# Two of the first unit's seven classical chunks mixed by block products, and their token-matrix groups narrowed in earlier chunks

## The chip, the cores and the metric

The kernel runs on one core of one Trainium2 chip. The metric is the device time of one execution in microseconds (us); lower is better. A core has TensorE (PE, with its weight loads shown as PEld), VectorE (DVE), ScalarE (ACT), GpSimd (POOL) and SyncE (SP), which here issues most of the DMAs.

## The reference

`x` is 8 x 3008 x 256. The first half is a spectral layer (transform along the 3008 tokens, complex 256x256 mix, soft threshold, transform back); the second is a mixer block on its result `y`:

```python
X = np.fft.rfft(x, axis=1)
Yr = Xr @ w_r - Xi @ w_i + b_r
Yi = Xr @ w_i + Xi @ w_r + b_i
Yr, Yi = soft_threshold(Yr, 0.01), soft_threshold(Yi, 0.01)
y = np.fft.irfft(Yr + 1j * Yi, n=3008, axis=1)
...
h = np.maximum(y.T @ w_tok1, 0) @ w_tok2      # along tokens, 256 wide inside
u = y + h.T
out = u + np.maximum(u @ w_ch1, 0) @ w_ch2    # along channels, 1536 wide inside
```

## The kernel before, in words

Batches are taken in five units: batch 0, batch 1, and three pairs. Of each unit the spectral part (names `p`, `px`, `pm`, `pi`, `gp` on TensorE) must be done before its channel mixing can start. The channel mixing of a unit walks over *chunks* of tokens. A product in full precision is three matmuls of high and low parts (`mm3`).

There are two ways to mix a chunk. A **classical** chunk (`channel(n)`, at most 512 columns) makes, for each of 12 slices f of the inner width, `ph` (6 matmuls), its relu `hh` on ACT with the rest `hlo` on DVE, and `po` (6 matmuls): 144 matmuls of the chunk's width. A **wide** chunk (`channel7`, 940 to 1024 columns) cuts both weight layers and the chunk into quarters and uses seven block products instead of eight (`sx`, `sw`, `sy`, `sz`, `l` on TensorE, operands `op` and `ts` made by DVE, ACT and POOL): 6 pairs of slices x 2 layers x 7 products x 3 = 252 matmuls of half the chunk's width. In `channel7` the order of TensorE is the order of the code.

Before a chunk can be mixed its `u` must be made, by *groups* of 4 or 5 slots (376 or 470 columns) that don't line up with wide chunks. `half_u(g, ct)` is one half of group g: 6 matmuls with the group's token matrix (`wt2`), then small ones with `b2`, 10 rows of the profile for 5 slots. Both `wt2` and `b2` have one buffer each, so the loads of group g+1 go out on SP when group g has been used (`load_group(g + 1)` behind the second half). The table `needs` says which groups a chunk needs; `when` and `spots` in `channel7` say beside which step a half is made: with three groups, the spots for the second wide chunk are behind `N5` and `N7` of the first step, behind `N1` of the next, and then behind whole pairs of slices.

The token matrix comes as 64-bit floats. In the first unit each group is loaded raw, narrowed (`narrow`: 2 operations of ACT and 6 of DVE for each of two halves), split into high and low parts (`split_wt2`: ACT, then DVE) and written back to DRAM by `keep_wt2`; later units reload it from there. The raw tiles share the buffers "ld" (four) with the loads `x` and `a2` of the spectral part, the narrowed ones the buffers "o" with the spectral part's `xh` and `xl`.

The order of the work: a start of 157 us; then the classical chunks of unit 0, between whose slices the driver at the end of the program deals out the spectral steps of unit 1 and some of unit 2, at a `pace` of so much spectral work per classical work; then, before the last classical chunk, all the rest of the spectral work alone ("pure"); then the last classical chunk, in which the block weights are summed (`weigh`, `replace`) and the first groups for the first wide chunk are made; then wide chunks to the end. A scheduler turns this into the order of each engine, so work may be moved by some places. Before, chunks 0 to 6 are classical (470, 376, 376, 376, 470, 470, 470 columns) and chunk 7 (960) is the first wide one.

Of the kernel before, what the change touches and what calls it, by code (L numbers as in the profile page):

```python
# [29 lines left out]
TOKS = 2 * N1  # L30
# [5 lines left out]
NF = DF // 128  # L36
# [101 lines left out]
def tile_kernel(ctx: ExitStack, tc: tile.TileContext, io):  # L138
# [17 lines left out]
    def split(hi, lo, src, hi_eng, lo_eng):  # L156
        if hi_eng is S:
            S.copy(out=hi, in_=src)  # L158
        else:
            hi_eng.tensor_copy(out=hi, in_=src)  # L160
        lo_eng.tensor_tensor(out=lo, in0=src, in1=hi.bitcast(F32), op=ALU.subtract)  # L161
# [59 lines left out]
    wc = {"wt2": wk}  # L221
# [219 lines left out]
    def fetch_g(u):  # L441
        gts[u] = [const.tile([128, 2, len(UNITS[u]), C], F32R, name=n, tag=n) for n in ("gh", "gl")]
        for i, g in enumerate(gts[u]):
            DMA.dma_start(out=g.rearrange("p j b c -> p (j b c)").bitcast(F32), in_=g_d[u][i, :, :2 * len(UNITS[u]) * C])
# [440 lines left out]
    for u, bs in enumerate(UNITS):  # L885
        total, at = N * len(bs), 0
        if u == 0:
            widths = [k * TOKS for k in sizes[u]]
        else:
            widths = [total % CW7] + [CW7] * (total // CW7)  # L890
        for cw in widths:
            chunks.append((u, at, cw))
            at += cw
        assert at == total
# [17 lines left out]
    def load_wt2(g, pool=None, parts=(0, 1)):  # L912
        u, _, s, k = groups[g]
        cols = slice(s * TOKS, (s + k) * TOKS)
        if u == 0:
            for jt in parts:
                wfs.setdefault(g, {})[jt] = load_raw(io["wt2"][0, jt][:, cols], k * TOKS, pool)
        else:
            w = wc["wt2"].tile([128, 4, 480], F32R, name="wt2", bufs=1)
            DMA.dma_start(out=w[:, :, :k * TOKS].bitcast(F32), in_=wt2_d[:, :, cols])  # L920
            wts[g] = w

    def narrow_wt2(g, parts=(0, 1)):
        for jt in parts:
            wfs[g][jt] = load_wide(None, wfs[g][jt].shape[1], raw=wfs[g][jt])

    def keep_wt2(g):
        u, _, s, k = groups[g]
        if u == 0:
            DMA.dma_start(out=wt2_d[:, :, s * TOKS:(s + k) * TOKS], in_=wts[g][:, :, :k * TOKS].bitcast(F32))  # L930

    def split_wt2(g, parts=(0, 1)):
        n = groups[g][3] * TOKS
        if g not in wts:
            wts[g] = wk.tile([128, 4, 480], F32R, name="wt2", bufs=1)
        for jt in parts:
            split(wts[g][:, jt, :n], wts[g][:, 2 + jt, :n], wfs[g].pop(jt), S, V)

    def load_b2(g):
        u, b, s, k = groups[g]  # L940
# [53 lines left out]
    def channel(n):  # L994
# [26 lines left out]
        for f in range(NF + 2):  # L1021
# [11 lines left out]
            if after:  # L1033
                mine = needs[n + 1]
                seven = after[2] > CW
                if f == 1 and seven:
                    yield "rest of it"
                    open_seven()
                    fetch_g(after[0])
                    load_wt2(mine[0])  # L1040
                    load_b2(mine[0])
                if f == 2 and not seven:
# [6 lines left out]
                    replace((0, f // 4))  # L1049
                if seven and f % 4 == 1 and f > 1:  # L1050
                    replace((1, f // 4 - 1))
                first_at, apart = (9 if len(mine) == 1 else 4 if seven else 6), (3 if seven else 4)
                for i, g in enumerate(mine):
                    if not seven and f in (1, 3, 4, 5, 6):
# [73 lines left out]
    def replace(key):  # L1128
        layer, q = key
        if layer == 0:  # L1130
            cols = slice(q * 512, (q + 1) * 512)
            h, l = (wc["w1"][:, k, 0, cols].rearrange("m (p i f) -> m p i f", p=2, i=2)[:, :, 1] for k in range(2))
        else:
            h, l = (wc[k][:, 4 * q:4 * q + 4][:, 0::2, 128:] for k in ("w2h", "w2l"))
        split(h, l, kept.pop(key), S, V)
# [372 lines left out]
```

## Time and profile before

| | |
|---|---|
| median of 3 runs | 2316.3 us (2315.58 to 2317.71) |
| the profiled execution | 2314.35 us, span 2312.2 us |
| PE / PEld busy | 98% / 85% |
| DVE / ACT / POOL busy | 74% / 64% / 60% |
| mean granted clock | 0.997 |
| end of classical chunks 0 to 5 (the `po` sums) | 198.7, 234.5, 277.7, 329.3, 389.7, 450.8 us |
| spectral work alone | about 452 to 850 us |
| last classical chunk; wide chunks | 850 to 907 us; 907 us to the end |

Busy shares are shares of the span. The duration of a matmul in a row overlaps the next one, so matmuls are counted below by the distance of their starts.

### The profile page before, as it was taken

What the parts mean: (1) busy time and instruction counts of PE and PEld (TensorE: products, weight loads), DVE (VectorE), ACT (ScalarE), POOL (GpSimd) and SP (SyncE); (2) the same over time, 40 slices, a digit from 0 to 9 for tenths busy, and PEclk for the clock granted to TensorE, in tenths of its full rate; (3) what the DMA queues carried; (4) which work ended last, traced back from release to release, by engine and by line L of the source; (5) the groups of instructions that cost most, each with busy time, mean ns of one, the idle gap of its engine ahead of it and who ended that gap; (6) DMA issues with size and microseconds to landing.
All of it is one profiled execution on the core that took longest, in us unless ns stands there. A gap on an engine that the chain in (4) does not pass through costs nothing.

```text
span 2312.2 us, 34805 instructions
## 1 busy us (share of the span) xinstructions
PE 2272.1 (98%) x12092; PEld 1975.2 (85%) x12092; DVE 1718.3 (74%) x2806; ACT 1476.5 (64%) x2700; POOL 1387.5 (60%) x1118
## 2 busy tenths in 40 slices
PE   8999999999999999999999999999999999999998
PEld 7769999989989988888988888898888889888876
DVE  7967776577887667777777777777777777777877
ACT  6655454455555445776676777667777766767776
POOL 0000222344553433887787888778788877878885
PEclk9999999999999999999999999999999999999999
DMA  8776566787876542122222212222221122222101
GB/s 219 240 251 182 144 196 196 231 264 246 274 238 211 186 153 89 41 81 69 84 62 69 64 34 69 70 85 62 69 65 43 60 69 85 62 69 64 59 1 37
DMA packets 150957, 277.22 MB, mean 120 GB/s; under 512 B 11077, under 2 KB 95389, under 8 KB 150781
## 3 DMA queue, kind: packets, MB, share of 16 engines
q1 hardware_dynamic: 115241, 208.40, 30.1%
q10 hardware_dynamic: 35540, 66.60, 8.6%
q8 instruction: 96, 1.57, 0.3%
q14 instruction: 80, 0.66, 0.1%
HBM read 177.57 MB, written 97.39 MB: 119 GB/s over the span
## 4 chain that ended last, share of the span: by engine, by line
PE 83%; DVE 9%; DMA 3%; issue 2%; ACT 2%; SPq 1%; POOL 1%; ACTq 0%; DVEq 0%; POOLq 0%
PE l L134 15%; PE sx L134 14%; PE sz L134 11%; PE sy L134 10%; PE sw L134 7%; PE px L497 3%; PE pm L208 2%; PE pm L210 2%; PE pm L209 2%; PE gp L210 1%; PE gp L208 1%; PE gp L209 1%; DMA raw<-in_wt 1%; DVE ts L1216 1%; PE ph L209 1%
## 5 line engine op out<-in xcount | busy, mean ns | idle before, releaser
L1213 POOL TENSOR_TENSOR op<-ts,op 128x512 fp32r<-128x512 f32 (+2 forms) x503 | 638.0, 1290 | 243.5 <-ACT op L1246 239.9
L1246 ACT ACTIVATE op<-ts 128x512 fp32r<-128x512 f32 (+2 forms) x504 | 311.2, 619 | 62.6 <-DVE ts L1216 47.9
L1213 DVE TENSOR_TENSOR uf<-sy,uf 128x512 f32<-128x512 f32 (+2 forms) x232 | 156.1, 673 | 222.5 <-PE sy L134 222.0
L134 PE MATMUL l<-op,ws 128*128 128x512 f32 (+2 forms) x1134 | 314.3, 385 | 0.0
L134 PEld LDWEIGHTS l<-op,ws 128*128 128x128 f32 x1134 | 212.9, 188 | 40.1
L1242 ACT ACTIVATE x<-sx 128x512 f32<-128x512 f32 (+2 forms) x252 | 148.5, 589 | 139.2 <-PE sx L134 138.7
L134 PE MATMUL sx<-ub,w 128*128 128x512 f32 (+2 forms) x756 | 211.2, 388 | 2.0 <-DVE ts L1216 1.2
L134 PE MATMUL sx<-ub,ws 128*128 128x512 f32 (+2 forms) x756 | 209.8, 386 | 0.5 <-ACT x L1242 0.5
L161 POOL TENSOR_TENSOR yl<-z,yh 128x512 fp32r<-128x512 f32 x72 | 96.2, 1336 | 125.8 <-ACT yh L158 121.9
L134 PEld LDWEIGHTS sx<-ub,w 128*128 128x128 f32 x756 | 141.4, 188 | 31.6 <-DVE ts L1216 3.5
L134 PEld LDWEIGHTS sx<-ub,ws 128*128 128x128 f32 x756 | 141.9, 188 | 27.8 <-ACT x L1242 0.9
L1213 POOL TENSOR_TENSOR op<-b,op 128x512 fp32r<-128x512 f32 (+2 forms) x126 | 160.6, 1274 | 0.7 <-ACT op L1246 0.2
L1213 DVE TENSOR_TENSOR x<-sw,x 128x512 f32<-128x512 f32 (+2 forms) x126 | 85.7, 680 | 90.3 <-PE sw L134 89.1
L262 POOL TENSOR_TENSOR sd<-x 120x512 f32<-120x512 f32 x39 | 60.8, 1558 | 151.5 <-DVE xl L161 108.2
L208 PE MATMUL pm<-wmh,xth 128*128 128x256 f32 x504 | 145.5, 289 | 2.9 <-DVE z L541 1.6
L1266 ACT ACTIVATE x<-x 128x512 f32<-128x512 f32 (+2 forms) x126 | 78.6, 624 | 108.5 <-DVE x L1213 108.5
L134 PE MATMUL sy<-op,w2h 128*128 128x512 f32 (+2 forms) x464 | 142.0, 387 | 1.4 <-DVE uf L1213 1.4
L210 PE MATMUL pm<-wmh,xtl 128*128 128x256 f32 x504 | 142.5, 283 | 0.0
L209 PE MATMUL pm<-wml,xth 128*128 128x256 f32 x504 | 142.5, 283 | 0.0
L161 POOL TENSOR_TENSOR xtl<-xs,xth 128x256 fp32r<-128x256 f32 x84 | 69.8, 831 | 105.1 <-ACT xth L158 58.7
L161 POOL TENSOR_TENSOR wt<-aw,wt 128x512 fp32r<-128x512 f32 x12 | 16.3, 1361 | 181.9 <-ACT wt L158 181.9
L506 DVE TENSOR_TENSOR xtl<-px,xth 128x512 fp32r<-128x512 f32 x84 | 57.7, 687 | 71.5 <-ACT xth L505 55.5
(225 smaller groups left out, 6679.0 us busy)
## 6 DMA issues: line engine op xcount, KB each, us to landing
wt<-wt_d SPq DMA_DIRECT2D x28, 940.0 KB, 5.6
x<-in_x SPq DMA_DIRECT2D x39, 480.0 KB, 5.6
a<-a_d SPq DMA_DIRECT2D x36, 512.0 KB, 5.9
wt<-ws_d SPq DMA_DIRECT2D x36, 512.0 KB, 4.8
b_d<-bt ACTq DMA_DIRECT2D x36, 512.0 KB, 5.8
a_d<-a ACTq DMA_DIRECT2D x36, 480.0 KB, 4.1
wt<-wt_d SPq DMA_DIRECT2D x21, 752.0 KB, 5.2
b<-b_d SPq DMA_DIRECT2D x32, 480.0 KB, 6.3
```

The costliest lines, as they stand in the source:

```text
L134: return lambda *args, **kw: self.tc.keep_in_program_order(op(*args, **kw))
L161: lo_eng.tensor_tensor(out=lo, in0=src, in1=hi.bitcast(F32), op=ALU.subtract)
L208: PE.matmul(out, lhsT=wh, rhs=xh, start=start, stop=False, skip_group_check=more)
L209: PE.matmul(out, lhsT=wh, rhs=xl, start=False, stop=False, skip_group_check=more)
L210: PE.matmul(out, lhsT=wl, rhs=xh, start=False, stop=stop, skip_group_check=more)
L262: eng.tensor_tensor(out=sd[:, 0], in0=x[:, 0], in1=x[:, 1], op=ALU.add)
L497: PE.matmul(pt[:, o:o + 128], lhsT=x, rhs=f2cols(2 * kp + ab), start=True, stop=True)
L506: V.tensor_tensor(out=v(xl)[:, 1:], in0=both, in1=v(xh)[:, 1:].bitcast(F32), op=ALU.subtract)
L1213: eng.tensor_tensor(out=out, in0=in0, in1=in1, op=op)
L1242: pins[key] = S.activation(out=t, in_=src, func=func)
L1246: pins[k] = S.activation(out=ops[k][:, 0], in_=v[k] if src is None else src, func=AF.Copy if k[0] == "t" else AF.Relu)
L1266: pins["x2r"] = S.activation(out=v["x2"], in_=v["x2"], func=AF.Relu)
```

## The change

Chunks 5 and 6 of before become one wide chunk 5 of 940 columns, the first wide one. So chunk 4 is now the last classical chunk, the spectral steps are dealt out over chunks 0 to 3 instead of 0 to 5, and chunk 4 makes groups 5 and 6 (of unit 0), where the last classical chunk before made groups 7, 8 and 9 (of unit 1). Groups 5 and 6 are now loaded, narrowed, split and kept beside chunks 1 and 2, in addition to those chunks' own groups, and reloaded from DRAM later. The low parts of the split of all groups but the first move from DVE to POOL.

```diff
         if u == 0:
-            widths = [k * TOKS for k in sizes[u]]
+            widths = [k * TOKS for k in sizes[u][:5]]
+            widths.append(total - sum(widths))
...
     def load_wt2(g, pool=None, parts=(0, 1)):
-        if u == 0:
+        if u == 0 and "seven" not in wc:
...
     def split_wt2(g, parts=(0, 1)):
-            split(wts[g][:, jt, :n], wts[g][:, 2 + jt, :n], wfs[g].pop(jt), S, V)
+            split(wts[g][:, jt, :n], wts[g][:, 2 + jt, :n], wfs[g].pop(jt), S, G if g else V)
...
     def channel(n):
                 if f == 1 and seven:
                     yield "rest of it"
                     open_seven()
-                    fetch_g(after[0])
+                    if after[0] != u:
+                        fetch_g(after[0])
                     load_wt2(mine[0])
                     load_b2(mine[0])
...
+                spare_g = {1: 5, 2: 6}.get(n)
+                if spare_g and f in (6, 8):
+                    load_wt2(spare_g, parts=[f // 2 - 3])
+                if spare_g and f in (8, 10):
+                    narrow_wt2(spare_g, parts=[f // 2 - 4])
+                if spare_g and f in (11, 13):
+                    split_wt2(spare_g, parts=[f // 2 - 5])
+                if spare_g and f == NF + 1:
+                    keep_wt2(spare_g)
+                    del wts[spare_g]
```

Three places show how the instructions move. On TensorE, the first wide chunk before: the stage begins with the seven products of the first step (`sx`, `sw`, `sx`, `sw`, `sy`, `sx`, `sx`), the first of the second layer (`l`) and the first of the next step; then comes the first half of the next group (`sz<-wt`).

```order
L134 MATMUL sx<-ub,w_963 128x480 x3
L134 MATMUL sw<-ub,ws 128x480 x3
L134 MATMUL sx<-ub,ws 128x480 x3
L134 MATMUL sw<-ub,w_963 128x480 x3
L134 MATMUL sy<-ub,w_963 128x480 x3
L134 MATMUL sx<-ub,ws 128x480 x3
L134 MATMUL sx<-ub,w_963 128x480 x3
L134 MATMUL l<-op,w2h 128x480 x2
L134 MATMUL l<-op,w2l 128x480
L134 MATMUL sx<-ub,w_963 128x480 x3
L134 MATMUL sz<-wt_9423,gh 128x470 x2
```

The same engine and place after the change, from the fifth product on (the first half of group 7, on the tile `wt_8939`, stands behind the first two products; `wt_9094` is group 8):

```order
L134 MATMUL sy<-ub,w_963 128x470 x3
L134 MATMUL sx<-ub,ws 128x470 x3
L134 MATMUL sz<-wt_8939,gh 128x470 x2
L134 MATMUL sz<-wt_8939,gl 128x470
L134 MATMUL sz<-wt_8939,gh 128x470 x2
L134 MATMUL sz<-wt_8939,gl 128x470
L134 MATMUL sz<-g_78,b_8941 128x94 x5
L134 MATMUL sx<-ub,w_963 128x470 x3
L134 MATMUL l<-op,w2h 128x470 x2
L134 MATMUL l<-op,w2l 128x470
L134 MATMUL sx<-ub,w_963 128x470 x3
L134 MATMUL sz<-wt_9094,gh 128x470 x2
```

Two halves now stand among the first seven products, and only nine matmuls lie between the last use of group 7 and the first of group 8, whose loads wait for that last use.

On DVE, where chunk 0 ends, before: the sum of chunk 0 (`uf<-po`) stands between the split of one group of unit 1 (`xl`) and the sums of another, with `hlo` of chunk 1 ahead of the next `xl`.

```order
L177 TENSOR_SCALAR wide<-wide 128x376
L179 SCALAR_TENSOR_TENSOR wide<-wide 128x376
L161 TENSOR_TENSOR xl<-sd,xh 120x512
L1076 TENSOR_TENSOR uf<-po,uf 128x2x470
L262 TENSOR_TENSOR sd<-x 120x256
L263 TENSOR_TENSOR sd<-x 120x256
L180 TENSOR_SCALAR wide<-wide 128x376
L1012 SCALAR_TENSOR_TENSOR hlo<-ph,hh 128x376
L161 TENSOR_TENSOR xl<-sd,xh 120x512
```

After:

```order
L262 TENSOR_TENSOR sd<-x 120x256
L263 TENSOR_TENSOR sd<-x 120x256
L161 TENSOR_TENSOR xl<-sd,xh 120x512
L1088 TENSOR_TENSOR uf<-po,uf 128x2x470
L262 TENSOR_TENSOR sd<-x 120x256
L263 TENSOR_TENSOR sd<-x 120x256
L161 TENSOR_TENSOR xl<-sd,xh 120x512
L262 TENSOR_TENSOR sd<-x 120x256
L263 TENSOR_TENSOR sd<-x 120x256
L161 TENSOR_TENSOR xl<-sd,xh 120x512
```

The groups of unit 1 now follow each other with nothing between; on TensorE the products with the `xl` behind the sum come right behind the last `po` of chunk 0.

On TensorE, where chunk 1 ends, before: of its last 18 `po` the middle and the end, followed by `ph` of chunk 2.

```order
L208 MATMUL po<-hh,w2h 128x376
L209 MATMUL po<-hlo,w2h 128x376
L210 MATMUL po<-hh,w2l 128x376
L208 MATMUL po<-hh,w2h 128x376
L209 MATMUL po<-hlo,w2h 128x376
L210 MATMUL po<-hh,w2l 128x376
L208 MATMUL ph<-uh,w_963 128x376
```

After:

```order
L208 MATMUL po<-hh,w2h 128x376
L209 MATMUL po<-hlo,w2h 128x376
L210 MATMUL po<-hh,w2l 128x376
L208 MATMUL p_2212<-xh,f1r 128x512
L209 MATMUL p_2212<-xl,f1r 128x512
L210 MATMUL p_2212<-xh,f1r 128x512
L208 MATMUL p_2217<-xh,f1r 128x512
L209 MATMUL p_2217<-xl,f1r 128x512
L210 MATMUL p_2217<-xh,f1r 128x512
L497 MATMUL px<-f_77,a_2149 128x128 x4
L208 MATMUL po<-hh,w2h 128x376
```

Spectral products of units 2 and 1 now stand between the last `po` of chunk 1.

## The prediction

> **What bounds the kernel now.** I read the page first, then a table by stage, then TensorE's rows where the change puts its hands.
>
> ```profile
> span 2312.2 us, 34805 instructions
> ...
> PE 2272.1 (98%) x12092; PEld 1975.2 (85%) x12092; DVE 1718.3 (74%) x2806; ACT 1476.5 (64%) x2700; POOL 1387.5 (60%) x1118
> ```
>
> The stages (columns: length, then PE, PEld, DVE, ACT, POOL busy, granted clock, DMA share, GB/s):
>
> ```profile
> core 0: us, PE busy (x) PEld busy (x) DVE busy (x) ACT busy (x) POOL busy (x), PEclk, DMA share, GB/s
> ...
> 157.00:452.00 295.00, 288.32 (x1723) 269.58 (x1723) 208.83 (x353) 148.44 (x283) 65.75 (x51) 0.99 0.62 187
> 452.00:849.60 397.60, 394.82 (x2609) 358.53 (x2610) 300.39 (x496) 215.36 (x429) 186.01 (x164) 1.00 0.70 227
> ...
> 907.00:2312.20 1405.20, 1391.92 (x6682) 1180.72 (x6680) 1047.62 (x1643) 987.72 (x1760) 1115.04 (x889) 1.00 0.20 61
> ```
>
> TensorE is the bound in every stage: it idles 6.7 of 295 us beside the classical chunks 0 to 5, 2.8 of 398 us in the spectral work alone. So a matmul taken away is time saved, as long as no new wait of TensorE takes its place. Where the last classical chunk meets the first wide one the distances and the waits are:
>
> ```profile
> 904.52 0.38 PE L208 MATMUL po<-hh,w2h 128*128 128x470 f32 x1
> ...
> 906.87 0.37 PE L210 MATMUL po<-hh,w2l 128*128 128x470 f32 x1
> 907.08 0.82 PE L134 MATMUL sx<-ub,w 128*128 128x480 f32 x3
> ...
> 909.07 0.92 PE L134 MATMUL sx<-ub,ws 128*128 128x480 f32 x3 [0.52 <-ACT x L1242]
> ...
> 912.70 0.91 PE L134 MATMUL sx<-ub,w 128*128 128x480 f32 x3 [0.76 <-DVE sw L1213]
> ...
> 915.23 0.93 PE L134 MATMUL sx<-ub,w 128*128 128x480 f32 x3 [0.62 <-DVE ts L1216]
> 916.00 0.58 PE L134 MATMUL sz<-wt,gh 128*128 128x470 f32 x2
> ...
> 918.30 0.89 PE L134 MATMUL sw<-ub,ws 128*128 128x480 f32 x3
> ...
> 919.68 0.81 PE L134 MATMUL sx<-ub,ws 128*128 128x480 f32 x3
> 920.33 0.81 PE L134 MATMUL sw<-ub,w 128*128 128x480 f32 x3
> ```
>
> From 904.52 to 907.08 stand twelve classical matmuls: 0.213 us each for 470 columns. In the wide chunk three of 480 columns take 0.65 us, 0.217 each, the same per column. So 0.213 is the price of a 470-column matmul of either kind.
>
> **The change part by part.**
>
> *The products.* Two classical chunks of 470 go: 2 x 144 = 288 matmuls. One wide chunk of 940 comes: 252 of 470. That is 36 fewer, 36 x 0.213 = **-7.7 us**, all on the engine that bounds. Scaling the 480-column rows instead (0.212) gives -7.9. The groups' halves only move: one group less in each of two classical chunks, one less in the last one, three more in the wide stage, each as long as before. DVE, ACT and POOL work of the wide chunk stays beside TensorE, as in the other wide chunks, where TensorE is busy 1392 of 1405 us.
>
> *The start of the wide stage.* Before, 27 matmuls from 907.08 to 916.00 take 8.92 us, where 27 x 0.217 = 5.85 would do: 3.07 us are lost to the chain of ACT and DVE on a stage that has just begun (the three waits named, and shorter ones). Now two halves of group 7, 2.3 us each (916.00 to 918.30 is such a half), stand inside this chain and fill those waits: -3.07. But then group 8 is due nine matmuls, 9 x 0.213 = 1.9 us, behind the last use of group 7's single buffers. How long a reload takes shows in the last classical chunk before: the queue of SP, TensorE's rows there, the weight loads' wait, and the landing times.
>
> ```profile
> 878.58 0.57 SPq L920 DMA_DIRECT2D wt<-wt_d  x1
> 879.67 0.33 SPq L942 DMA_DIRECT2D b<-b_d  x1
> ```
>
> ```profile
> 878.39 1.25 PE L965 MATMUL pu<-g,b 96*128 96x94 f32 x10
> 879.42 0.46 PE L208 MATMUL ph<-uh,w 128*128 128x470 f32 x1
> ```
>
> ```profile
> 885.87 0.30 PEld L965 LDWEIGHTS pu<-g,b 96*128 96x128 f32 x2 [0.21 <-DMA b<-b_d]
> ```
>
> ```profile
> wt<-wt_d SPq DMA_DIRECT2D x28, 940.0 KB, 5.6
> ...
> b<-b_d SPq DMA_DIRECT2D x28, 480.0 KB, 6.3
> ```
>
> Call 879.42 the end of the old group, T. The matrix is issued at T-0.84 and lands 5.6 us later, at T+4.8; `b` is issued at T+0.25 and is seen to land at T+6.45, where even 24 matmuls between the groups were just too few (the 0.21). In the new order TensorE comes at T+1.9, or T+2.5 if the chain of the first step still delays the `sx` before it; it waits over 2 us for the matrix, then does six matmuls (1.3 us), then waits for `b` until T+6.45. Without waits `b` would be used at T+1.9+1.3 = T+3.2: **3.25 us** lost, which takes back the 3.07. Behind TensorE, in program order, the whole wide stage is queued, so nothing hides it. Bounds for start and reload together: -3.1 (loads land in time) to +3.3 (the first waits stay as well, at least in part); I take +0.2, since both are read from rows of the same operations.
>
> *The clock.* A short idle time can cost more than itself:
>
> ```profile
> 230.75 0.34 PE L210 MATMUL po<-hh,w2l 128*128 128x376 f32 x1
> 232.64 0.43 PE L208 MATMUL po<-hh,w2h 128*128 128x376 f32 x1 [1.55 <-ACT hh L1011]
> ...
> 234.21 0.52 PE L208 MATMUL ph<-uh,w 128*128 128x376 f32 x1
> 234.52 0.52 PE L209 MATMUL ph<-ul,w 128*128 128x376 f32 x1
> ...
> 238.17 0.33 PE L208 MATMUL ph<-uh,w 128*128 128x376 f32 x1
> 238.34 0.33 PE L209 MATMUL ph<-ul,w 128*128 128x376 f32 x1
> ```
>
> ```profile
> 873.52 0.48 PE L209 MATMUL po<-hlo,w2h 128*128 128x470 f32 x1 [1.41 <-DVE hlo L1012]
> ```
>
> Behind a wait of 1.55 us the starts are 0.31 us apart from 234.21 on, against 0.17 for this width, until about 237.6: some 3.4 us at half speed, 1.7 us lost. Behind one of 1.41 us at 873.52 the distance stays 0.21. The new wait of 2.2 us and its half us for `b` lie above both: I take +1.4 of the 1.7 (bounds 0 and 1.7). The Trainium skill, page "TensorE: Matmul & The Clock Gate", section "What's actually happening", says the clock falls back after an idle window of about 3.4 us; by that neither this wait nor the one below would cost any clock, and the sum would be 3 us lower. The trace differs, with half speed behind 1.55 us.
>
> *The classical stage.* Its spectral work now falls on four chunks instead of six. TensorE's share of it is only moved, and what it needs of DVE comes closer together:
>
> ```profile
> 198.73 1.13 DVE L1076 TENSOR_TENSOR uf<-po,uf 128x940 f32<-128x940 f32 x1
> 199.77 0.41 DVE L262 TENSOR_TENSOR sd<-x 120x256 f32<-120x256 f32 x1
> 200.11 0.42 DVE L263 TENSOR_TENSOR sd<-x 120x256 f32<-120x256 f32 x1
> ...
> 201.21 0.69 DVE L161 TENSOR_TENSOR xl<-sd,xh 120x512 fp32r<-120x512 f32 x1
> ```
>
> ```profile
> 199.59 0.28 PE L208 MATMUL p<-xh,f1r 120*128 120x256 f32 x1
> 199.71 0.28 PE L209 MATMUL p<-xl,f1r 120*128 120x256 f32 x1
> ```
>
> ```profile
> L161 POOL TENSOR_TENSOR yl<-z,yh 128x512 fp32r<-128x512 f32 x72 | 96.2, 1336 | 125.8 <-ACT yh L158 121.9
> ```
>
> ```profile
> L1012 DVE SCALAR_TENSOR_TENSOR hlo<-ph,hh 128x470 fp32r<-128x470 f32 x36 | 23.1, 643 | 18.9 <-ACT hh L1011 18.9
> ...
> L161 DVE TENSOR_TENSOR wt<-wide,wt 128x470 fp32r<-128x470 f32 x6 | 4.7, 776 | 1.6 <-ACT wt L158 1.5
> ...
> L161 DVE TENSOR_TENSOR wt<-wide,wt 128x376 fp32r<-128x376 f32 x6 | 4.1, 686 | 0.6 <-ACT wt L158 0.6
> ```
>
> In bulk DVE still fits. From 208.8 us go 24 `hlo` x 0.643 = 15.4, two sums of 1.13, and 12 low parts (4.7 + 4.1 = 8.8) that move to POOL: 182. The stage shortens by 61.4 (288 x 0.213) and two groups of 4.6 to some 224 us: 81% instead of 71%. POOL has 65.8 us there and gains twelve operations; the nearest POOL row, 128x512, is 1.34 us on the page, 16 us at most. DMA goes from a share of 0.62 to some 0.8, which the spectral stage's 0.70 nearly has.
>
> Locally one place does not fit. At the end of chunk 0 the sum `uf<-po` needs the last `po`, and behind it on DVE stand two `sd` and the `xl` that TensorE wants as its very next matmul but one: from 198.73 those take 1.13 + 0.34 + 0.34 + 0.69, less small overlaps, 2.4 us, so TensorE waits some 2.6 us, and 0.8 more for the next `xl` (each group costs DVE 1.4 us, TensorE 6 x 0.12 = 0.7). With 1.6 for the clock: +5.0. Against it, the 1.55 us wait at the end of chunk 1, with 0.5 of shorter gaps and its 1.7 of clock, goes: spectral products now stand between the `po` there: -3.8. The other waits of the stage I leave as they are. Together **+1.2**, bounds -4 (the new place costs nothing) to +6 (DVE late at several chunk ends).
>
> *Costed at nothing.* Loading, narrowing and splitting groups 5 and 6 is moved, not added; the reload in the last classical chunk stands 24 matmuls behind the group before it, as it did before. The spare loads stand in SP's queue ahead of unit 2's first `x` and unit 1's `a2`; that wait is a rival below.
>
> **Sum.** -7.7 + 0.2 + 1.4 + 1.2 = -4.9 us. On the profiled execution's 2314.35 us that is 2309.4; the median of the runs lies 1.95 us above that execution, so the forecast is **2311.3 us**.
>
> **The rivals.**
>
> *Both new waits stay hidden.* The chain of the first step may hold back the products ahead of group 8, or DVE may be ready at chunk 0's end. For it speak the 24-matmul spacing that cost 0.21 us only; against it that nine matmuls are 3.2 us short. Then -7.7 - 3.1 or -7.7 - 3.8 and some of the rest: about 2306 us. Chance 0.12.
>
> *DVE becomes the bound between classical slices.* 81% in the mean hides stretches above 100%, such as chunk 0's end; three more waits like the one at 230.75, 1.55 + 1.7 with its clock less often, would take back 3 to 6 us: 2312 to 2317, no change that can be told. The page "SBUF — State Buffer" of the Trainium skill, section "SBUF: two separate sides", has POOL and a two-input DVE operation lock each other out; by it the twelve moved operations could cost DVE up to those 16 us again, which is this rival. For it: the thin places above. Against it: the spectral stage runs at 76% of DVE (300 of 398) and TensorE idles only 2.8 us there. Chance 0.39.
>
> *The load buffers run dry, and it is slower.* The spare raw tiles take two of four "ld" buffers in chunks 1 and 2, and SP waits for them in order:
>
> ```profile
> SPq L475 <- DVE wide L181: 13.6, 4, 9.4
> ```
>
> Already now SP's loads of `a2` waited 13.6 us in four waits for narrowing on DVE. Four more spare halves could double that; it decides once a wait outlasts the lead of `a2`, about one step of unit 1 (some 12 us). If 13.6 us came through: 2311.3 + 13.6 = 2325. Against it, none of the present waits, up to 9.4 us, reached TensorE. Chance 0.07.
>
> **How the numbers follow.** Forecast (gain of 4.6 to 8 us) 0.42, first rival 0.12, second 0.39, third 0.07. About 0.2% (4.6 us) can be told from no change, so faster is 0.42 + 0.12 = 0.54, same 0.39, slower 0.07. The range reaches to the first rival, 2306, and to the end of the second, 2317; the forecast's own is 2308.3 to 2311.7.
>
> **What would show it.** Products: 36 fewer matmuls, distances of 0.213. Reload: a wait of over 2 us at the third `sz<-wt` half, put down to the DMA of `wt` or `b`, and half speed behind it. Classical stage: a wait of some 2.6 us for `xl` at the start of chunk 1, none at its end. I am wrong if the classical stage has many waits for DVE or DMA, or if the reload shows no wait.

## The result: 13 us slower, and the profile after

| | before | after |
|---|---|---|
| median, 4 runs each (lowest to highest) | 2316.89 us (2315.58 to 2317.71) | 2329.78 us (2329.05 to 2330.39) |
| the profiled execution | 2314.35 us, span 2312.2 | 2330.39 us, span 2328.6 |

The ratio is 1.0063, with a 95% interval of 1.0051 to 1.0075: slower by 0.6%, where 0.2% faster was forecast and 2317 was the upper end of the range. From the page of the changed kernel, span and busy times:

```profile
span 2328.6 us, 34964 instructions
...
PE 2274.8 (98%) x12056; PEld 1970.2 (85%) x12056; DVE 1749.2 (75%) x2842; ACT 1504.8 (65%) x2754; POOL 1459.6 (63%) x1173
```

TensorE has 36 matmuls fewer, as the arithmetic says, and is busy 2.7 us longer. To find the place, both executions are cut at the same five points of the program: the first `ph`, the first `ph` of the last classical chunk, the first `sx`, and one and the same `sx` of a later wide chunk. Columns as in the stage table above. Before, then after:

```profile
0.00:156.91 156.91, 140.97 (x786) 117.03 (x786) 121.53 (x253) 100.97 (x184) 3.23 (x6) 0.99 0.82 239
156.91:849.64 692.73, 683.26 (x4332) 628.24 (x4333) 509.31 (x848) 363.89 (x711) 251.80 (x215) 1.00 0.67 210
849.64:907.08 57.44, 56.03 (x296) 49.24 (x295) 39.89 (x65) 23.92 (x46) 17.42 (x9) 1.00 0.46 144
907.08:1372.44 465.36, 463.20 (x2246) 395.22 (x2244) 342.42 (x541) 327.59 (x589) 366.51 (x294) 1.00 0.21 62
1372.44:2312.20 939.76, 928.65 (x4437) 785.44 (x4436) 705.13 (x1102) 660.13 (x1172) 748.53 (x596) 1.00 0.20 60
```

```profile
0.00:161.42 161.42, 142.51 (x787) 117.60 (x787) 122.94 (x254) 101.05 (x184) 3.23 (x6) 0.98 0.82 235
161.42:793.75 632.33, 617.00 (x3981) 566.07 (x3982) 489.90 (x805) 347.45 (x683) 269.76 (x227) 0.99 0.71 226
793.75:850.76 57.01, 52.80 (x264) 44.48 (x263) 41.77 (x67) 23.04 (x43) 19.04 (x9) 1.00 0.41 128
850.76:1388.70 537.94, 533.54 (x2593) 456.71 (x2591) 389.43 (x616) 372.99 (x674) 418.15 (x337) 1.00 0.21 64
1388.70:2328.60 939.90, 928.94 (x4436) 785.28 (x4436) 705.15 (x1102) 660.29 (x1172) 749.41 (x596) 1.00 0.20 60
```

Each row is read against the TensorE work that was moved, at 0.2133 us for a 470-column matmul and 4.6 us for a group (two halves of 2.3):

| stretch | length after minus before | work moved | left over |
|---|---|---|---|
| start, the same instructions | +4.5 | 0 | +4.5 |
| classical stage and spectral work alone | -60.4 | -61.4 - 2 groups (9.2) = -70.6 | **+10.2** |
| last classical chunk | -0.4 | one group, -4.6 | **+4.2** |
| first wide chunks | +72.6 | 252 x 0.2133 + three groups = +67.6 | **+5.0** |
| the rest | +0.1 | 0 | +0.1 |

The moved work sums to -7.6, the rest to +24. The 4.5 us at the start are not the change: over the profiles of all the kernels below, the first `ph` comes at 156.9 to 162.2 us with seven classical chunks and at 157.9 to 161.4 with five. (So the two profiled executions lie 16.0 us apart, the medians 12.9.) The other three places hold +19.4.

**The classical stage.** The largest single place in it is the end of chunk 0. TensorE, then DVE and ACT, in the changed kernel:

```profile
203.81 0.28 PE L210 MATMUL p<-xh,f1r 120*128 120x256 f32 x1
205.78 0.38 PE L208 MATMUL p<-xh,f1r 120*128 120x256 f32 x1 [1.69 <-ACT xh L158]
206.51 0.45 PE L209 MATMUL p<-xl,f1r 120*128 120x256 f32 x1 [0.35 <-DVE xl L161]
...
209.00 0.58 PE L208 MATMUL p<-xh,f1r 120*128 120x256 f32 x1 [1.19 <-ACT xh L158]
209.38 0.52 PE L208 MATMUL ph<-uh,w 128*128 128x376 f32 x1
```

```profile
203.17 1.14 DVE L1088 TENSOR_TENSOR uf<-po,uf 128x940 f32<-128x940 f32 x1
204.23 0.41 DVE L262 TENSOR_TENSOR sd<-x 120x256 f32<-120x256 f32 x1
204.56 0.42 DVE L263 TENSOR_TENSOR sd<-x 120x256 f32<-120x256 f32 x1
```

```profile
205.11 0.62 ACT L158 CAST xh<-sd 120x512 fp32r<-120x512 f32 x1 [0.40 <-DVE sd L263]
207.85 0.58 ACT L284 COPY a<-p 120x512 f32<-120x512 f32 x1 [2.12 <-PE p L210]
208.33 0.62 ACT L158 CAST xh<-sd 120x512 fp32r<-120x512 f32 x1
```

Groups of unit 1's first transform stand here with no classical matmul between them, and the two long waits have different reasons. Ahead of the first (1.69 us), DVE makes the sum of chunk 0 and then the two `sd` of the group; ACT's `xh` at 205.11 waits for the second `sd`, not for ACT's copy of the group before, which had ended at 204.71. That is the chain of the prediction. The second (1.19 us) is a ring: `xh` on ACT, `xl` on DVE, six `p` on TensorE, the copy `a` on ACT, and only behind that copy the next `xh`. From 205.11 to 208.33 it takes 3.2 us, part of it at half clock. The same ring with the same waits at full clock, in two of the runs below, takes 2.8 us from one `p` to the next, in which the six `p` need 0.7. In the kernel before, such groups came at 199.59, 202.39 and 205.18:

```profile
202.39 0.28 PE L208 MATMUL p<-xh,f1r 120*128 120x256 f32 x1
...
205.18 0.28 PE L208 MATMUL p<-xh,f1r 120*128 120x256 f32 x1
```

That is 2.8 us apart too, but with twelve classical matmuls (2.1 us) between two groups, and TensorE did not wait. Behind the waits after the change the clock falls to half. The granted clock (third column from the end) in stretches of the changed kernel, first here, then behind the reload of group 8:

```profile
206.00:213.00 7.00, 5.46 (x21) 5.01 (x21) 4.26 (x10) 2.74 (x5) 0.00 (x0) 0.55 0.85 244
...
865.00:869.00 4.00, 3.07 (x10) 2.74 (x11) 0.00 (x0) 0.00 (x0) 2.46 (x3) 0.57 0.35 74
```

That is 3.2 us lost in the first window (3.4 with the next us: the clock over 200 to 220 us is 0.83) and 1.7 behind the reload. Over the span the mean granted clock, 0.997 before, is now

```profile
core 0: 2328.6 us, clock 0.995
```

so that 0.3% of 2312 us were lost to it before and 0.5% of 2329 after, 6.9 and 11.6 us, each uncertain by 1.2 since the clock is given to 0.001. The four runs of the changed kernel have 0.993 to 0.995, the runs of the kernel before 0.995 to 0.998.

The rest of the stage matters as much. Waits of TensorE and half speed (taken from the granted clock), before and after:

| place | before | after | difference | forecast |
|---|---|---|---|---|
| chunk 0 up to 190 us | 2.9 | 2.6 | -0.3 | 0 |
| end of chunk 0 | 0.8 | 6.6 | +5.9 | +5.0 |
| end of chunk 1 | 3.3 | 0 | -3.3 | -3.8 |
| the other waits from 213 to 460 us | 3.0 | 8.6 | **+5.6** | 0 |
| spectral work behind it | 2.5 | 2.0 | -0.6 | 0 |

The figures are rounded one by one. They sum to +7.3 of the +10.2; the other 3 us stand in no listed wait. Behind 213 us there were three waits, and there are ten now, of 0.3 to 1.5 us. Six of them, 4.2 us, are put down to DVE (`z`, `hlo`, `xs`, `uf`); the longest, 1.5 us for POOL's `wt` at 375.55, has 1.7 us of half speed behind it.

One wait of chunk 0 has its reason on POOL. The first of the low parts that the change gave to POOL takes 3.68 us there instead of 1.0 to 1.3 as the next ones, beside dense work of DVE; ACT's next operation waits for it, and behind that `hh`, `hlo` and TensorE come late:

```profile
178.98 3.68 POOL L161 TENSOR_TENSOR wt<-wide,wt 128x376 fp32r<-128x376 f32 x1 [24.12 <-ACT wt L158]
...
182.69 0.66 ACT L172 ACTIVATE wide<-raw 128x512 f32<-128x512 f32 x1 [2.89 <-POOL wt L161]
...
186.90 0.48 PE L209 MATMUL po<-hlo,w2h 128*128 128x470 f32 x1 [1.85 <-DVE hlo L1013]
```

**The last classical chunk and the wide start.** The waits of TensorE from 793.75 to 880 us (in total, times, longest):

```profile
PE po L209 <- DVE hlo L1013: 3.3, 5, 1.1
PE sz L134 <- DMA wt<-wt_d: 2.1, 1, 2.1
PE sx L134 <- ACT x L1254: 1.1, 1, 1.1
PE po L208 <- ACT hh L1012: 0.9, 2, 0.6
PE sx L134 <- DVE ts L1228: 0.7, 1, 0.7
```

Before, `hlo` cost 1.41 us here, once. It now costs 3.3 in five waits. Two, 0.81 and 0.65 us before 830 us, stand beside the sums of the block weights, as did the one before the change. The reason for the other three, 1.09, 0.47 and 0.29 us from 842 us on, stands in DVE's rows, with one of POOL:

```profile
837.49 1.94 DVE L1170 TENSOR_TENSOR t<-uf 128x470 f32<-128x470 f32 x1 [0.46 <-ACT uf L972]
840.08 0.65 DVE L161 TENSOR_TENSOR ub<-t,ub 128x470 fp32r<-128x470 f32 x1 [0.65 <-ACT ub L158]
840.64 0.64 DVE L1176 TENSOR_TENSOR t<-uf 128x470 f32<-128x470 f32 x1
...
841.88 0.64 DVE L1013 SCALAR_TENSOR_TENSOR hlo<-ph,hh 128x470 fp32r<-128x470 f32 x1
```

```profile
837.09 1.84 POOL L161 TENSOR_TENSOR ws<-sf,ws 128x768 fp32r<-128x768 f32 x1 [1.90 <-ACT ws L158]
```

The operands of the first wide chunk (`t`, `ub`) are made as soon as its last group is. That was group 9, at slice 10 of the last classical chunk; it is now group 6, at slice 7, so they stand ahead of the last four `hlo` in DVE's order. At the wide start the reload waits where it was expected, and half speed follows:

```profile
862.88 0.92 PE L134 MATMUL sx<-ub,w 128*128 128x470 f32 x3 [0.69 <-DVE ts L1228]
865.93 1.12 PE L134 MATMUL sz<-wt,gh 128*128 128x470 f32 x2 [2.14 <-DMA wt<-wt_d]
866.85 0.59 PE L134 MATMUL sz<-wt,gl 128*128 128x470 f32 x1
867.24 0.99 PE L134 MATMUL sz<-wt,gh 128*128 128x470 f32 x2
```

From 866.85 to 867.24 is 0.39 us for one matmul of 0.213.

### The profile page after: what moved, and what is told of

It reads as the page before. It is cut to its first block, busy times and chain, and to the rows that moved or that the text cites. A ratio compares the mean times of both kernels' runs of the same rounds, so it can differ in the third digit from the quotient of the medians.

```text
span 2328.6 us, 34964 instructions
## 1 busy us (share of the span) xinstructions
PE 2274.8 (98%) x12056; PEld 1970.2 (85%) x12056; DVE 1749.2 (75%) x2842; ACT 1504.8 (65%) x2754; POOL 1459.6 (63%) x1173
## 4 chain that ended last, share of the span: by engine, by line
PE 78%; DVE 10%; DMA 5%; ACT 2%; issue 2%; POOL 1%; SPq 1%; ACTq 0%; DVEq 0%; POOLq 0%
PE l L134 15%; PE sx L134 14%; PE sz L134 11%; PE sy L134 10%; PE sw L134 8%; PE px L497 2%; PE pm L208 2%; PE pm L210 2%; PE pm L209 2%; PE gp L210 1%; PE gp L208 1%; PE gp L209 1%; DVE ts L1228 1%; DMA raw<-in_wt 1%; DVE ub L160 1%
## 5 line engine op out<-in xcount | busy, mean ns | idle before, releaser
L1225 POOL TENSOR_TENSOR op<-ts,op 128x512 fp32r<-128x512 f32 (+3 forms) x527 | 667.2, 1289 | 259.8 <-ACT op L1258 256.1
L1258 ACT ACTIVATE op<-ts 128x512 fp32r<-128x512 f32 (+3 forms) x528 | 325.7, 618 | 67.7 <-DVE ts L1228 52.1
L1225 DVE TENSOR_TENSOR uf<-sy,uf 128x512 f32<-128x512 f32 (+3 forms) x243 | 163.4, 672 | 236.2 <-PE sy L134 235.8
L134 PE MATMUL l<-op,ws 128*128 128x512 f32 (+3 forms) x1188 | 328.7, 385 | 0.0
L1254 ACT ACTIVATE x<-sx 128x512 f32<-128x512 f32 (+3 forms) x264 | 155.3, 588 | 144.5 <-PE sx L134 143.8
L134 PE MATMUL sx<-ub,w 128*128 128x512 f32 (+3 forms) x792 | 220.9, 387 | 1.4 <-DVE ts L1228 1.3
L134 PE MATMUL sx<-ub,ws 128*128 128x512 f32 (+3 forms) x792 | 219.5, 385 | 1.1 <-ACT x L1254 1.1
L1225 POOL TENSOR_TENSOR op<-b,op 128x512 fp32r<-128x512 f32 (+3 forms) x132 | 168.3, 1275 | 1.6 <-ACT op L1258 1.1
L134 PE MATMUL sy<-op,w2h 128*128 128x512 f32 (+3 forms) x486 | 148.7, 387 | 1.4 <-ACT t L1319 1.1
L134 PEld LDWEIGHTS sz<-g,b 96*128 96x128 f32 x896 | 114.8, 192 | 3.1
```

The lines of the kernel that those rows point to most:

```text
L134: return lambda *args, **kw: self.tc.keep_in_program_order(op(*args, **kw))
L1225: eng.tensor_tensor(out=out, in0=in0, in1=in1, op=op)
L1254: pins[key] = S.activation(out=t, in_=src, func=func)
L1258: pins[k] = S.activation(out=ops[k][:, 0], in_=v[k] if src is None else src, func=AF.Copy if k[0] == "t" else AF.Relu)
```

## The experiments

Each was timed against the kernel before on the same chip; the ratio is to that, with its 95% interval (the changed kernel: 1.0063, 1.0051 to 1.0075). The median of the kernel before itself lay between 2314.1 and 2316.9 us in the sets of runs, so the intervals decide.

### The wide start

Group 8 later:

```diff
-spots = [... for p in ['N5', 'N7', (1, 'N1'), 1, 2, 3] ...]
+spots = [... for p in ['N5', 'N7', 1, (2, 'N5'), 2, 3] ...]
```

> The changed kernel with the first half of group 8 made two pairs of slices later, so that 36 matmuls instead of nine stand between the last use of group 7's buffers and the first use of group 8's. Theory "sum of places" (the loss is made of separate waits of TensorE, each worth what its rows show): the 2.14 us wait at the third half and the 3.4 us of doubled distances behind it (1.5 us) go, 2329.8 - 3.6 = about 2326. Rival "the wait only moves" (TensorE is a little ahead of DVE and ACT in the first wide steps and waits there next): 2329 to 2330, with new waits for DVE or ACT of 2 us or more in the first two steps.

Measured 2326.49 us, 1.0042 (1.0030 to 1.0055). The reload wait and its half speed are gone from the trace, and no wait over 1.1 us took their place. The size is that expected, though its interval and that of the changed kernel overlap a little.

No half of a group in the first step:

```diff
+spots = [... for p in [(1, 'N1'), 1, 2, (3, 'N1'), 3, (4, 'N1')] ...]
```

> The changed kernel with no half of groups 7 to 9 in the first wide step; all six stand in steps 1 to 4, each group 36 or more matmuls behind the one before. So no reload wait, as in the run with group 8 alone moved (2326.5), but the waits of the first step are no longer filled. If two halves there fill 3.07 us, as the prediction had it, this is 2329 to 2330, with the three waits of before (0.52, 0.76, 0.62) back at the start. If they fill little, because ACT's copies for those halves delay the x that TensorE waits for, 2326 to 2327.

Measured 2322.90 us, 1.0038 (1.0025 to 1.0050): below both times that were expected, and not slower than the run above, so two halves in the first step fill nothing. Two of the three waits of before are back at the start, 0.75 and 0.62; with the halves there, ACT copies the result of one ahead of the `x` that TensorE wants, which costs the 1.1 us above. The rows give the same loss either way: from the first `sx` to the end of the 27 matmuls that the prediction counts it takes 8.2 us without the halves and 12.8 with them (4.6 of it the halves), where the 27 need 5.8; 2.4 us are lost in both.

### The last classical chunk

```diff
-    V.scalar_tensor_tensor(out=hlo, ...)
+    hs["rest"] = V.scalar_tensor_tensor(out=hlo, ...)
...
-if f in (10, 11) and seven:
-    (first_u if f == 10 else rest_u)(n + 1)
+if f in (12, 13) and seven:
+    with tc.issue_after(hs["rest"].ins): (first_u if f == 12 else rest_u)(n + 1)
```

> The changed kernel with the operands of the first wide chunk (t and ub) held back behind the hlo of slice 11, instead of being taken as soon as group 6 is made. Theory "sum of places": the waits of po for hlo in the last classical chunk (3.3 us over five, 0.9 for hh) shrink to one of 1.4 or less as before, -3 to -4 us; the operands come later and the first wide step loses 1 to 3 of that: 2326 to 2329. Rival "the weight sums cause them" (weigh, weigh2, replace stand in the same slices of a chunk that is one step shorter of other work): the waits stay at 3 us or more and the time at 2329.8 or above.

Measured 2323.56 us, 1.0032 (1.0020 to 1.0044). The waits for `hlo` fall from 3.3 to 0.7 us and those behind 840 us are gone, so the operands did cause these, but the price of that is seen in the waits of the same stretch:

```profile
PE sx L134 <- ACT x L1254: 2.8, 1, 2.8
PE sz L134 <- DMA wt<-wt_d: 1.7, 1, 1.7
```

Six of the seven copies `ub` on ACT now come between 843 and 850 us, the last right ahead of the first `x`. Half speed follows both waits (5.1 us by the granted clock from 845 to 870 us), which takes back what the last classical chunk gained (52.2 us instead of 57.0); the median, 6 us below that of the changed kernel, gained more than this trace shows.

Both, with `b11` and `t1` left early (the edit of group 8, and only `rest_u` held back):

```diff
+if f == 10 and seven: first_u(n + 1)
+if f == 12 and seven:
+    with tc.issue_after(hs["rest"].ins): rest_u(n + 1)
```

> The changed kernel with group 8 two pairs later and with the last five operands of the first wide chunk (not b11 and t1) held back behind the hlo of slice 11. By the sum of places: reload and clock -3.6, the hlo waits of the last classical chunk -3 to -4, and some 1 us given back where the operands come late: 2323 to 2325. If waits only move, no better than either of the two alone, 2324 to 2327 with a wait for ACT's x of over 2.5 us in the first wide step.

Measured 2320.44 us, 1.0027 (1.0015 to 1.0039), clearly better than the changed kernel, and a little better than the sum of places. Some 8 (by the ratios) to 9 us (by the medians) can be taken back at these two places. The classical stage and the spectral work behind it are in its trace as long as in the changed kernel, 632.8 us against 632.3, so the 10.2 us lost there are what is left. Holding back the operands together with the empty first step:

> The changed kernel with no half of groups 7 to 9 in the first wide step (2322.9 alone) and the last five operands of the first wide chunk behind the hlo of slice 11. If the losses of the last classical chunk and of the wide start add up: 2322.9 - 3 = 2320, no wait for hlo over 1 us after slice 5, and the three waits of before at the start (0.5 to 0.8). If the later operands hold up the first step, now that no group's half stands in it, 2322 to 2324.

Measured 2326.79 us, 1.0048 (1.0036 to 1.0060), slower than either forecast: TensorE waits 3.25 us for ACT's first `x`, against 1.6 in the run before, where a group's half stood ahead of it. Such a half fills nothing as the change has it, but it does when the operands come late.

### Chunks 0 to 3

Thinner, with the rest of unit 1's steps alone:

```diff
-left_s = UNIT1 - spent
+left_s = 0.66 * (UNIT1 - spent)
```

> The changed kernel with two thirds of the spectral work dealt out over chunks 0 to 3, that is at the density that the kernel before has over its six, the rest alone behind chunk 3. Theory "density": the excess of TensorE's time over its dense matmuls in chunks 0 to 3 and the spectral stage, 38.8 us after against 28.6 before, falls back by 6 to 10: 2320 to 2324. Rival "the extra narrowing of groups 5 and 6 is what makes DVE and ACT late": 2327 to 2330, with the waits of chunks 1 and 2 as they are and only that at the end of chunk 0 changed.

Measured 2339.31 us, 1.0100 (1.0086 to 1.0113): 10 us slower still. The wait at the end of chunk 0 is nearly gone, but unit 1's later steps, now behind the classical chunks, wait for the splits of their weights. From 340 to 430 us:

```profile
PE gp L210 <- POOL wt L161: 7.0, 3, 4.1
PE p L208 <- DVE xs L507: 2.1, 1, 2.1
PE gp L208 <- ACT wt L158: 1.6, 1, 1.6
```

So neither theory holds: put behind the classical chunks, unit 1's later steps are short of TensorE work beside them too. Groups 5 and 6 narrowed beside the spectral work alone:

```diff
-spare_g = {1: 5, 2: 6}.get(n)
+spare_g = None
...
+for g, at in ((5, 60), (6, 100)):     # i counts the spectral steps
+    for jt in range(2):
+        if i == at + 10 * jt: load_wt2(g, parts=[jt])
+        if i == at + 10 * jt + 5: narrow_wt2(g, parts=[jt])
+        if i == at + 10 * jt + 10: split_wt2(g, parts=[jt])
+    if i == at + 25: keep_wt2(g)
```

> The changed kernel with groups 5 and 6 loaded, narrowed, split and kept beside the spectral work alone instead of beside chunks 1 and 2. Theory "density": chunks 1 to 3 lose about 5 us more than before in the changed kernel, most of it to the spectral work, so this gives 1 to 2 us: 2328. Rival "extra narrowing": 2324 to 2326, with the waits of chunks 1 to 3 gone and the spectral stage as long as it was.

Measured 2341.14 us, 1.0106 (1.0092 to 1.0120), 11 us over the changed kernel, which neither theory had. A stretch in which DVE was busy 76% before had no room for this: from 400 to 660 us TensorE waits 5.7 us for DVE's `z` alone. The narrowing left out:

```diff
-spare_g = {1: 5, 2: 6}.get(n)
+spare_g = None
...
-DMA.dma_start(out=wt2_d[:, :, s * TOKS:(s + k) * TOKS], in_=...)
+for at in [s] + ([s + k, s + 2 * k] if g == 4 else []):
+    DMA.dma_start(out=wt2_d[:, :, at * TOKS:(at + k) * TOKS], in_=...)
```

> The changed kernel without the loading, narrowing and splitting of groups 5 and 6: group 4's matrix, which has the same width, is stored in their two places as well, so that part of the computation is left out; the stores and the reloads remain. It weighs the narrowing beside chunks 1 and 2 against the lost cover. Theory "narrowing" (DVE and ACT are late because chunks 1 and 2 carry two groups each): 2321 to 2324, with TensorE's excess between 209 and 450 us down by 5 or more. Theory "lost cover" (unit 1's spectral steps have 288 fewer classical matmuls between them, and the groups don't matter): 2327 to 2329, with the waits at the end of chunk 0 and those for POOL's wt and DVE's z as they are.

Measured 2328.64 us, 1.0059 (1.0045 to 1.0073), the same as the changed kernel: where the change put it, the narrowing costs nothing that can be told. The same narrowing alone, in the kernel before:

```diff
+spare_g = {1: 5, 2: 6}.get(n)
...
+if g in early_kept:
+    DMA.dma_start(out=w[:, :, :k * TOKS].bitcast(F32), in_=wt2_d[:, :, cols])
```

> The kernel before (seven classical chunks) with one part of the change alone: groups 5 and 6 are narrowed beside chunks 1 and 2, kept, and reloaded beside chunks 4 and 5; the density of the spectral work is as before. Theory "lost cover": at most the price of a few short waits in chunks 1 and 2, 0 to +3 us against before. Theory "narrowing": +5 to +8.

Measured 2320.15 us, 1.0025 (1.0014 to 1.0036). It does cost there: in chunks 1 and 2 are single waits of 3.1 us for `hh` and 2.2 for `hlo`, where the longest of before in chunks 0 to 3 are 1.55 and 1.07. So its price is not additive, and why it vanishes beside the tighter packing was not settled. The low parts of the groups on DVE again:

```diff
-split(..., S, G if g else V)
+split(..., S, V)
```

> The changed kernel with the low parts of all groups on DVE again, as before. If POOL's new twelve operations hold up POOL's split of the spectral weights (TensorE's 1.5 us wait of gp for wt at 375 us), this gives 1 to 3 us, 2327 to 2329. If DVE is the one that is short beside the classical chunks, this costs: 8.8 us more of DVE there, 2331 to 2334, with longer waits for hlo and z.

Measured 2328.10 us, 1.0059 (1.0045 to 1.0072): no difference that can be told, either way. Its trace lacks the wait of 1.85 us in chunk 0, as does that of the run without a half in the first step, where POOL's first low part took 1.0 us; but it has one of 3.06 us for `hlo` at 273.70. So POOL's operations can hold up TensorE, but they don't decide the time.

That leaves the packing. The kernel before, with it alone:

```diff
-left_c = mixing(0, first_wide - 1)
+left_c = mixing(0, 4)
```

> The kernel before (seven classical chunks, no early narrowing, no wide chunk more) with unit 1's spectral work dealt over chunks 0 to 3 instead of 0 to 5, which gives TensorE the same steps in chunks 0 to 2 as the changed kernel has; chunks 4 and 5 then stand beside the next unit's steps. Theory "packing" (a classical slice with more spectral work beside it makes DVE and ACT late, whatever else is changed): the waits of the changed kernel at the end of chunk 0 (1.7 + 1.2 us for xh) and of 0.5 to 2 us behind it come, +5 to +10 us against before. Theory "cover" (unit 1's spectral steps alone are slow, and what costs is that 288 classical matmuls are gone from the whole stage, wherever they stood): +0 to +3 us, because the matmuls are still there.

Measured 2325.04 us, 1.0042 (1.0028 to 1.0056), 9 us over the kernel before. Its waits from 190 to 215 us are those of the changed kernel to the tenth:

```profile
PE p L208 <- ACT xh L158: 2.9, 2, 1.7
PE p L209 <- DVE xl L161: 0.3, 1, 0.3
```

From the first `ph` to the last classical chunk it takes 700.3 us, where the kernel before takes 692.7. The theory "packing" stands: narrowing, reload and the wide chunk are not needed for this loss, and its 7.6 us are most of the 10.2. Starting 15 us earlier in chunk 0:

```diff
-pace, hold = 0.0, left_c - 25.0
+pace, hold = 0.0, left_c - 10.0
```

> The changed kernel with unit 1's spectral work starting after 10 us of chunk 0 instead of 25, so that 15 us more of classical matmuls stand beside it and chunks 0 to 3 carry it thinner (7.1 instead of 4.4 us of p in chunk 0, the rest a little less). Theory "packing": waits spread, 2326 to 2328. Theory "cover": the stage from 160 us to the last classical chunk gets 3 to 6 us shorter, 2323 to 2326. Rival "chunk 0 has no room": DVE is still narrowing w2 and group 1 there, new waits for hlo in chunk 0 eat it up, 2329 to 2332.

Measured 2340.50 us, 1.0114 (1.0095 to 1.0133): chunk 0 has no room, as the rival had it. It takes 58 us instead of 48, with waits for `xl` (2.1), `hlo` (1.4, 0.2) and `xh` (1.2, 1.2, 0.6).

Is it the ring? The same packing in the kernel before, with a group's price raised so that they come further apart:

```diff
-SLOW = 1.75
+SLOW = 3.0
```

> The kernel before with unit 1's steps over four chunks (325 us dense packing: 2325.0) and the same raised price for the first transform's groups. Theory "ring": the end of chunk 0 is as before again, 2325 - 5 = 2320. Rival "later steps": 2324 to 2327, with waits of gp for POOL's wt and of p for DVE's xs or z in chunk 3 and behind.

Measured 2318.70 us, 1.0015 (1.0007 to 1.0024), against 1.0042 without the price, and the intervals don't meet. The trace has no wait at all from 190 to 215 us, and the stretch from the first `ph` to the last classical chunk is 694.0 us, against 700.3. So two thirds of what the packing costs go away when the groups of the first transform come further apart. That this is the end of chunk 0 alone is not shown: the price enters the driver's sums, so the later steps move as well; the waits of the whole stretch sum to much the same (14 and 13 us), and what the trace has less of is half speed: none at all, where the run without the price lost 1.8 us at the end of chunk 0 and 1.7 behind 254 us. (The "325 us" in the recorded text is a slip: 2325.0 is meant.) The same price in the changed kernel:

> The changed kernel with the price of a group of unit 1's first transform in the driver's table raised from 1.75 to 3.0, so that four of them instead of six stand in chunk 0 behind its first 25 us, and eight instead of nine in chunk 1; the later steps (pm, pi, gp) come denser in chunk 2 and 3. Theory "ring" (a group takes 3.2 us from xh to xh, of which TensorE works 0.7, so it needs 2.5 us of other matmuls, and the changed kernel gives it 1.6 in chunk 0): the waits for xh at the end of chunk 0 (1.7, 0.35, 1.2) and the half speed behind them (3.4) go, 2329.8 - 5 = 2325. Rival "the later steps are as short of cover": what is won there is lost in chunks 2 and 3, 2328 to 2332.

Measured 2334.58 us, 1.0086 (1.0073 to 1.0099), not the ring's 2325 and even over the rival's 2328 to 2332. The end of chunk 0 has one wait of 0.58 us left, but with chunks 4 and 5 gone, what the first transform no longer uses up is missing further on. From 225 to 420 us:

```profile
PE px L497 <- ACT a L284: 5.0, 1, 5.0
PE p L209 <- DVE xl L161: 4.2, 1, 4.2
PE p L208 <- DVE hlo L1013: 3.3, 1, 3.3
```

Last, another engine for `xh`, which cuts the ring but not the chain from DVE's sum:

```diff
-split(xh, xl, sd, S, V)
+split(xh, xl, sd, G, V)
```

> The changed kernel with the high parts xh of unit 1's first transform made on POOL, which is idle there, instead of on ACT, where each stands behind the copy of the group before. By the ring: xh can run a group ahead, the two waits for xh at the end of chunk 0 go with their half speed, 2324 to 2327. If it is DVE (sum of chunk 0, sd, xl) that sets the pace there, the waits stay and are put down to DVE, 2329 to 2330; if POOL's copy is so long that the ring only changes engine (over 2 us), the same or worse.

Measured 2324.14 us, 1.0045 (1.0033 to 1.0057); the interval overlaps that of the changed kernel, so the time decides nothing. The trace does tell the two waits apart. The ring's (1.19) is gone, and no half speed follows; the first stays, with POOL's `xh` waiting for the `sd` behind DVE's sum:

```profile
203.85 0.62 POOL L160 CAST xh<-sd 120x512 fp32r<-120x512 f32 x1 [2.65 <-DVE sd L263]
...
204.52 0.39 PE L208 MATMUL p<-xh,f1r 120*128 120x256 f32 x1 [1.67 <-POOL xh L160]
```

With the other edits:

> The changed kernel with three edits together: group 8 two pairs later, the last five operands of the first wide chunk behind the hlo of slice 11 (these two gave 2320.4), and xh of the first transform on POOL (2324.1 alone). If the losses are separate, 2329.8 - 9.4 - 5.6 = about 2315, level with the kernel before. If xh on POOL gave only part of its 5.6 (its trace still has one wait for xh of 1.7 us at the end of chunk 0) or the same time is counted twice, 2318 to 2321.

> The changed kernel with no half of groups 7 to 9 in the first wide step (2322.9 alone) and xh of the first transform on POOL (2324.1 alone). Separate losses: 2329.8 - 6.9 - 5.6 = 2317. Otherwise 2320 to 2323.

Measured 2320.19 us, 1.0029 (1.0019 to 1.0038), and 2323.42 us, 1.0045 (1.0032 to 1.0057): nothing beyond the same kernels with `xh` on ACT (1.0027 and 1.0038). Moving `xh` gains nothing that can be told, and no version here beats the kernel before.

## Why the prediction was wrong, step by step

- **Products, -7.7: right.** 36 matmuls fewer, and the moved work in the table of stretches gives -7.6. (The -7.9 beside it is a slip: 36 x 0.212 is 7.6.)
- **Classical stage, +1.2 with bounds -4 to +6: the step that failed.** It measured +10.2, past its bound. The two places that were priced came out nearly as forecast, and for the reason given: the end of chunk 0 at 3.2 us of waits where 2.6 + 0.8 stood, the first behind DVE's sum and its `sd`, and the end of chunk 1 without its wait. What failed is the sentence "the other waits of the stage I leave as they are": DVE's mean share was taken for room, and all other places were put at nothing. They hold +5.6 us of waits and half speed from 213 to 460 us and some 3 us that stand in no listed wait. The kernel before with only its packing changed lost 9 us. The prediction counted the 288 matmuls as work and not as cover: 61 us were taken away that had stood between the chains of ACT, DVE and POOL. One such chain is the ring, the second wait at the end of chunk 0, which needs 2.1 us of other matmuls for each group; its groups 2.8 us apart stood in the trace of before.
- **Start of the wide stage, +0.2: half right, and too small.** The reload waited as forecast (2.14 us, put down to the DMA of `wt`, at the third half). That the two halves of group 7 would fill 3.07 us is refuted: 2.4 us are lost with them and without. Start and what follows measured +5.0, of which 1.7 is half speed, for which the next term has 1.4.
- **Clock, +1.4, and +1.6 less 1.7 in the classical stage: too small.** By the mean granted clock it is some 4.7 us, 1.7 of it ahead of the change, between 100 and 110 us. The end of chunk 0 alone, two waits of 1.69 and 1.19 us, cost 3.4 where 1.6 stood, and the wait for POOL's `wt` at 375 us another 1.7; behind the reload the forecast 1.4 was 1.7.
- **Not in the sum: the operands of the first wide chunk.** An earlier last group moves them ahead of the last `hlo`. The last classical chunk lost 4.2 us; holding them back, together with a later group 8, takes back 8 to 9 us.
- **Costed at nothing:** narrowing groups 5 and 6 in chunks 1 and 2, rightly (the run without it is no faster), and the low parts on POOL, rightly by the medians; in the trace they cost a wait of 1.85 us.
- **The rivals.** "DVE becomes the bound between classical slices" came nearest in its reason, many waits for DVE in places that the mean hides, but its end of 2317 was 13 us short. "The load buffers run dry" came nearest in the number, 2325, by luck: SP's waits of `a2` for narrowing shrank from 13.6 us to 5.3.

```profile
SPq L475 <- DVE wide L181: 5.3, 3, 2.2
```

What stays open: with both places mended (1.0027) the kernel is still slower than before, while it has 7.7 us less to do. What is left is the 10.2 us of the classical stage, in waits of 0.3 to 1.9 us between 180 and 460 us and the half speed behind them. That the packing makes them is shown in the kernel before; in the changed kernel no edit of the packing took them back (thinner, earlier and with the raised price all came out slower), so there it is argued from the traces.

## What to carry to other kernels

Work on the engine that bounds is also cover for chains that run beside it: before taking it away, find the chains (the same instruction at a steady distance, with other work between) and compare their time alone with the work that is left. A term put at "as before" needs a reason of its own. An engine's mean busy share says little of room: 76% of DVE had none for two groups, and spectral work or narrowing put thinner, earlier or elsewhere came out 5 to 11 us worse still. When a producer finishes earlier, look at what an in-order engine now does ahead of something urgent.

## What the runs showed of the hardware

The same reload wait cost half speed in one run and none in another. In the run without narrowing, the wait of 1.97 us for `wt` at 866.20 is followed by distances of 0.21, and the clock stays full:

```profile
865.00:869.00 4.00, 2.77 (x17) 2.31 (x18) 0.00 (x0) 0.12 (x1) 2.93 (x3) 1.00 0.49 102
```

In the changed kernel 2.14 us gave 0.57 in the same window. The three waits at the end of chunk 0 (1.69, 0.3 and 1.19 us) stand in ten of the traces: in eight the clock over 200 to 220 us is 0.83, in two (all seven classical chunks with the denser packing, and the low parts on DVE) it is 0.91, that is 3.4 us lost or 1.8. So equal waits can cost different amounts of clock, and the profiled runs of one edit can differ by several us. The Trainium skill, page "TensorE: Matmul & The Clock Gate", section "What's actually happening", says that activity is watched in a free-running window of some 3.4 us, so that the point at which the clock rises depends on where in the window the first matmul falls. Such a window fits these rows, which no run tests further. The table of that section has the clock at half after at least one idle window; the rows here differ, since a wait of 2.14 us was enough.

A subtraction on DVE that takes 0.64 us at 840.64 took 1.94 at 837.49, beside POOL's 1.84 us; and POOL's low part at 178.98 took 3.68 us instead of 1.0 to 1.3 beside dense work of DVE. The page "SBUF — State Buffer" of the Trainium skill, section "SBUF: two separate sides", has a DVE operation with two inputs there and a POOL operation that reads from there lock each other out for a whole instruction, and these rows agree; the prediction had cited it for the low parts moved to POOL, where a trace shows its price (the 1.85 us in chunk 0) and no median does.
